# Splitting keys and weights on other engines in an attention, experts and FFN kernel

## The chip, the cores and the metric

The kernel runs on one core of one Trainium2 chip. The metric is device time in microseconds of one execution, and the median of three runs of the kernel before is 1194.65 us (1193.66 to 1194.86). The engines are TensorE (PE in the profile), VectorE (DVE), ScalarE (ACT), GpSimd (POOL) and SyncE (SP, which here only issues transfers).

## The reference

Three stages follow one another on 2304 tokens of 512 features:

```python
scores = q @ k.T / 8                      # 4 batches x 8 heads, 576 x 576, head size 64
mask = scores >= kth_largest(scores, 32)  # 32 best of each row
x = softmax(where(mask, scores, -1e9)) @ v
logits = x @ w_gate + modality_bias[modality_id]
e = argmax(logits)                        # one of 8 experts for each token
x = softmax(logits)[e] * (relu(x @ w1[e]) @ w2[e])    # 512 -> 1024 -> 512
h = x @ w_in                              # 512 -> 2048
out = where(h >= 1, h, where(h <= -1, 0, (h + 1)**2 / 4)) @ w_out
```

Everything is in 32-bit floats.

## The kernel before, in words

**Low and high parts.** TensorE multiplies a reduced form of the 32-bit floats. Where more precision is wanted, an operand is split into a high part (a copy into that form, such as `kh`, `qh`, `w1h`) and a low part (the operand less its high part: `kl`, `ql`, `w1l`), and three products stand for one.

**Attention.** The 32 heads are worked in 16 pairs, `j` = 0 to 15. Each pair has 9 units of 128 query rows by 576 keys; two units make a group, and the loop over `g` (line 504) runs through 72 groups. In a group the order of work on every engine is the order in which the Python code issues it: `topk(g)` (line 237) on VectorE and GpSimd; `masks` and `out` for the groups before; the scores of the group four later, which ScalarE evacuates from PSUM as `s`; the transposes `pt` on TensorE of the group before and their evacuations `a` on ScalarE; then what the dictionary `later` holds for this group, the first two entries of it ahead of the exponentials `e` and the others behind them.

`topk` finds the 32nd largest of each row by repeated maxima (MAX8) and replacements on VectorE. To shorten the rows it first folds them (line 207): `big`, the larger of a row's two halves, then `c` and `lit2`, the larger and smaller of the halves of `big`. One fold serves two groups and is issued in every odd group, behind that group's first maxima (lines 252, 254, 256). The third piece, `lit`, is made by GpSimd with two integer operations (`less`, line 224, its operations at 228 and 234), one group ahead; in odd groups it waits for the fold by a written-out dependency. GpSimd also makes `nm` (line 257), on which ScalarE's `e` waits, and two small copies for each group (line 241).

**Preparing a pair.** `prep(j, g)` (line 373) puts the steps of pair `j` into `later`. `turn` (line 162) transposes k or q with five TensorE transposes into a PSUM tile of the pool `sp`, of which there are two, shared with the scores; ScalarE evacuates them as `kT` or `qT`, and q a second time as `qh`. `kparts` (line 174) makes `kh` on VectorE by a cast of `kT`; `krest` and `qrest` (lines 178, 182) make `kl` and `ql` on GpSimd (for pair 0 on VectorE). Both turns come in the even group `g - 2`, `kparts` in `g - 1`, `krest` and `qrest` in the even group `g`; the loads of pair `j + 1` are issued on SP in `g - 2`.

**End of a pair.** `xout` (line 340) scales a finished pair: two small operations on VectorE (lines 345, 346), which stand behind that group's maxima, then on GpSimd `x` (line 349) and twice `xtail` (line 354). It is put into the odd group after the pair's last output.

**Routing and experts.** The tokens of the first three batches are ranked by expert inside the loop (`rank1`, `rank1_rest`), the others behind it (`rank2`, line 813); their rows are scattered to DRAM by indirect transfers that GpSimd issues. Then the experts' steps run: `up` products with w1, `down` products with w2, in an order written out in `Experts.ops`. `go(n)` issues n of them, and ahead of each one `prepare` (line 1453) issues loads on SP and the split of a weight tile two uses ahead. `split1` (line 1375) makes `w1h` on ScalarE and `w1l` on GpSimd, or on VectorE for the small steps; `split2` makes `w2h` on ScalarE and `w2l` on VectorE. The activations' parts `hh` (ScalarE) and `hl` (VectorE) follow each `up`, and the next `up` needs the one PSUM bank `h` that they read.

While the first two steps run, `route_steps` (line 850) works out on VectorE which tiles of 256 rows each later step takes. It is a generator, and between its portions one product step is issued:

```python
            for _ in self.route_steps():
                M.go(1)
```

It consists of some 60 operations on tiles of 8 to 152 columns. Behind it stands a branch on `redo` (line 605), taken when a row's 32 largest were not all found; each engine reads the flag itself. Then follow the wide steps, and the FFN, whose weights are unpacked beside them.

Of the kernel before, what the change touches and what calls it, by code (L numbers as in the profile page):

```python
# [65 lines left out]
class Kernel:  # L66
# [32 lines left out]
    def attention(self, moe):  # L99
        nc, tc = self.nc, self.tc  # L100
        with ExitStack() as ctx:
# [12 lines left out]
            def nb(n):  # L114
                return n if P.deep else 1
# [57 lines left out]

            def kparts(j):
                hi = kq["kh", j] = P.kq.tile([128, S], F32R, name="kh", bufs=nb(2))
                nc.vector.tensor_copy(hi, kq["k", j])
# [196 lines left out]
            def prep(j, g, *eng):  # L373

                at(g - 2, turn, j, "k")
                at(g - 2, turn, j, "q")
                at(g - 1, kparts, j)
                at(g, krest, j, *eng)
                at(g, qrest, j, *eng)
# [13 lines left out]
            for j in range(1, len(pairs)):  # L393
                g = odd(9 * j // 2 - AHEAD) - 1
                prep(j, g)
                if j + 1 < len(pairs):
                    at(g - 2, load, j + 1)
# [75 lines left out]
            def after(g, d):  # L473
                for j, u in units[2 * d:2 * d + 2]:
# [5 lines left out]
                    elif u == 8:  # L480
# [4 lines left out]
                        if late:  # L485
                            first.setdefault(g + 1, []).append((xout, (j,)))
                        else:
                            at(odd(g + 2), xout, j)
# [87 lines left out]
            M.copy = None  # L576
# [9 lines left out]
            M.flush()  # L586


            def again(j):
                load(j)  # L590
                load_v(j, vtile(j))
                for nm in "kq":
                    turn(j, nm)
                kparts(j)
                krest(j)
                qrest(j)
                for u in range(9):
# [84 lines left out]
    def route_consts2(self):  # L682
# [7 lines left out]
        def iota(name, shape, pattern):  # L690
            t = rp.tile(shape, F32, name=name)
            nc.gpsimd.iota(t, pattern=pattern, base=0, channel_multiplier=0,
                           allow_small_or_imprecise_dtypes=True)
            return t
# [9 lines left out]
        self.early = rp.tile([128, E], F32, name="early")  # L704
# [99 lines left out]
    def rank1_rest(self):  # L804
# [6 lines left out]
        nc.vector.tensor_scalar(j, j, self.end1[:, E - 1:E], -float(CAP), op0=ALU.subtract, op1=ALU.mult)  # L811

    def rank2(self, oh):
# [21 lines left out]
        nc.vector.tensor_copy(self.n2, cnt)  # L835
# [14 lines left out]
    def route_steps(self):  # L850
# [9 lines left out]

        k1, k2 = self.k1, self.k2
        end = row("end")
        tt(end, self.pref, k2, op=ALU.add)
        tt(end, end, self.end1, op=ALU.subtract)
        ts(end, end, self.end1[:, E - 1:E], None, op0=ALU.add)

        small = row("small")
        stt(small, k2, -float(CAP), self.n1, op0=ALU.mult, op1=ALU.add)
        yield
        tt(small, small, self.n2, op=ALU.add)  # L870
# [8 lines left out]
        def halve():  # L879

            stt(two, self.jcap, -2.0 / CAP, left[:, :, None].to_broadcast(n), op0=ALU.mult, op1=ALU.add)
            ts(two, two, 2.0, None, op0=ALU.is_ge)
# [4 lines left out]
        tt(left, left, small, op=ALU.subtract)  # L887
        halve()
        yield
        stt(odd, pairs, -2.0, left, op0=ALU.mult, op1=ALU.add)  # L890
# [4 lines left out]
        own, mate = on[:, SMALL0], on[:, SMALL0 + 1]  # L895
        tt(own, one, small, op=ALU.mult)
        tt(small, small, own, op=ALU.subtract)
        yield
        self.prefix(nth, small, "3")
# [3 lines left out]
        tt(left, last, self.early, op=ALU.subtract)  # L903
        halve()
# [8 lines left out]
        stt(rest, cover, -2.0, rest, op0=ALU.mult, op1=ALU.add)  # L913
        self.prefix(nrest, rest, "6")
        yield
# [4 lines left out]
        twice = row("twice")  # L920
        ts(twice, pairs, 2.0, None, op0=ALU.mult)
        tt(on[:, a], kk[:, a], each(twice, 2 * PAIRS), op=ALU.is_lt)
        yield
        tt(on[:, d], kk[:, d], each(rest, DYN), op=ALU.is_lt)
        stt(on[:, both], kk[:, both], 0.0, on[:, both], op0=ALU.is_ge, op1=ALU.mult)
        tt(kk[:, a], kk[:, a], each(self.early, 2 * PAIRS), op=ALU.add)
        stt(cover, cover, 2.0, self.early, op0=ALU.mult, op1=ALU.add)
        yield
        tt(kk[:, d], kk[:, d], each(cover, DYN), op=ALU.add)
        ts(kk[:, ONE0], last, -1.0, None, op0=ALU.add)  # L930
        ts(kk[:, SMALL0:], each(k2, SMALL), -1.0, None, op0=ALU.add)

        far, jump = row("far", NTAB), row("jump")
        tt(jump, end, k2, op=ALU.subtract)
        tt(jump, jump, self.base1, op=ALU.subtract)
        yield
        tt(far, kk, each(k1, NTAB), op=ALU.is_ge)
        tt(far, far, each(jump, NTAB), op=ALU.mult)
        tt(kk, kk, far, op=ALU.add)
        yield  # L940
        tt(kk, kk, each(self.base1, NTAB), op=ALU.add)
        stt(kk, kk, -float(NOCHUNK), on, op0=ALU.add, op1=ALU.mult)
        ids = fin.tile([128, 2, NTAB], F32, name="ids")
        nc.vector.tensor_reduce(ids[:, 0], kk, axis=AX.X, op=ALU.add)
        yield
# [4 lines left out]
        yield  # L950
# [336 lines left out]
class Experts:  # L1287


    def __init__(self, kn, wk, pss, steps):  # L1290
        self.kn, self.nc, self.wk, self.pss = kn, kn.nc, wk, pss
        self.steps = steps
        self.copy, self.busy, self.wide = None, False, None
# [81 lines left out]
    def split1(self, k, copy=None):  # L1375
        if k < len(self.use1):
            h, l = self.spl1[k] = [self.wk.tile([128, KC, 128], F32R, name="w1" + x, bufs=3) for x in "hl"]
            st, f = self.use1[k]
            eng = self.nc.vector if self.use1[k][0].small else self.nc.gpsimd
# [352 lines left out]
```

## Time and profile before

| | |
|---|---|
| median of 3 runs | 1194.65 us |
| profiled execution: its time / span in the profile | 1193.16 us / 1191.3 us |
| busy in the span | PE 94%, DVE 70%, ACT 59%, POOL 49% |
| mean granted TensorE clock | 0.968 of full speed |
| attention loop / routing / experts / FFN | to about 500 us / 500 to 551 / 551 to 840 / from 840 |

Times in the profile count from the first instruction of the span. A busy TensorE is not one at its peak, since ends of matmuls are modelled. In a timeline the columns are start, duration, engine, line, operation, output<-inputs with shapes; in square brackets stands the idle time of the engine ahead of the instruction, and what released it. A duration reaches a little into the next instruction, so what an instruction costs its engine is read from start to start.

### The profile page before, as it was taken

How to read it: one execution, taken by the hardware profiler on the slowest of the kernel's cores; microseconds unless marked ns; L12 is line 12 of the kernel's file. 1: busy time of each engine (PE TensorE's matmuls, PEld its weight loads, DVE VectorE, ACT ScalarE, POOL GpSimd, SP SyncE). 2: the span in 40 equal slices, each digit the busy share in tenths (PEclk: the TensorE clock that was granted, in tenths of full speed). 3: DMA queues.
4: the chain of work that ended last, by engine and by line, in shares of the span. 5: the costliest groups of instructions: out<-in, count | busy, mean ns of one | idle time of the engine just before them, and what ended most of it. 6: DMA issues, size and time to landing. Idle time of an engine off the chain costs nothing. (4 is left out here: it accounts for less than half of the span.)

```text
span 1191.3 us, 24612 instructions
## 1 busy us (share of the span) xinstructions
PE 1120.5 (94%) x8900; PEld 953.4 (80%) x8901; DVE 836.1 (70%) x2539; ACT 703.5 (59%) x1246; POOL 581.6 (49%) x668
## 2 busy tenths in 40 slices
PE   8989989999999898778999999889999999999998
PEld 5877778777887787666888777778899999999897
DVE  6999999999999999786758988488322232323222
ACT  5888989989898897633665545345433333333322
POOL 2777777777777777642324546032322323232222
PEclk7899999989999998998999999999999999999999
DMA  4036554201121003365766565242100101010000
GB/s 90 14 116 214 177 183 143 51 13 31 40 49 24 15 17 125 99 185 166 261 211 219 172 222 195 74 133 72 53 1 27 28 1 53 1 54 1 27 1 27
DMA packets 120843, 106.67 MB, mean 90 GB/s; under 512 B 64384, under 2 KB 88960, under 8 KB 120704
## 3 DMA queue, kind: packets, MB, share of 16 engines
q1 hardware_dynamic: 116320, 94.67, 25.7%
q0 software_dynamic: 2880, 9.44, 2.3%
q8 instruction: 73, 1.20, 0.4%
q10 hardware_dynamic: 1504, 0.82, 0.2%
q14 instruction: 66, 0.54, 0.2%
HBM read 70.30 MB, written 34.60 MB: 88 GB/s over the span
## 5 line engine op out<-in xcount | busy, mean ns | idle before, releaser
L1214 POOL TENSOR_TENSOR gl<-g,gh 128x384 fp32r<-128x384 f32 x96 | 97.2, 1012 | 315.9 <-ACT gh L1213 296.1
L307 PE MATMUL tp<-nhuge,w 128*128 128x128 bf16 x720 | 139.7, 229 | 18.1 <-ACT w L296 18.1
L1208 ACT ACTIVATE c<-c,half 128x384 f32<-128x384 f32 x96 | 59.2, 617 | 162.2 <-DVE c L1207 162.2
L305 PE MATMUL tp<-ident,e 128*128 128x128 f32 x720 | 152.3, 301 | 2.1 <-ACT e L291 2.0
L1207 DVE TENSOR_SCALAR c<-h 128x384 f32<-128x384 f32 x95 | 52.8, 555 | 143.1 <-PE h L1065 143.1
L1062 PE MATMUL h<-xh,wih 128*128 128x384 f32 x380 | 129.9, 342 | 5.5 <-DVEq L1118 3.2
L305 PEld LDWEIGHTS tp<-ident,e 128*128 128x128 f32 x720 | 107.6, 149 | 30.9 <-issue 9.4
L1063 PE MATMUL h<-xh,wil 128*128 128x384 f32 x380 | 129.1, 340 | 0.0
L1373 POOL TENSOR_TENSOR w1l<-w1r,w1h 128x512 fp32r<-128x512 f32 x48 | 67.9, 1417 | 121.2 <-ACT w1h L1372 88.6
L271 DVE MAX8 m<-z 128x8 f32<-128x160 f32 x432 | 117.1, 312 | 0.0
L312 ACT ACTIVATE a<-tp 128x640 f32<-128x640 f32 x144 | 102.0, 709 | 24.3 <-PE tp L307 22.9
L1073 PE MATMUL y<-woh,gl 128*128 128x512 f32 x288 | 114.7, 398 | 0.8 <-POOL gl L1214 0.8
L1071 PE MATMUL y<-woh,gh 128*128 128x512 f32 x288 | 112.7, 391 | 2.6 <-ACT gh L1213 2.3
L1211 DVE TENSOR_TENSOR g<-c,h 128x384 f32<-128x384 f32 x95 | 52.6, 553 | 88.1 <-ACT c L1208 88.1
L1072 PE MATMUL y<-wol,gh 128*128 128x512 f32 x288 | 114.2, 396 | 0.0
L291 ACT ACTIVATE e<-s,nm 128x576 f32<-128x576 f32 x144 | 103.4, 769 | 10.8 <-POOL nm L257 10.8
L296 ACT ACTIVATE w<-s,m 128x576 bf16<-128x576 f32 x144 | 103.6, 773 | 10.1 <-DVE m L271 10.1
L228 POOL TENSOR_TENSOR lit<-s 128x576 int32<-128x576 int32 x66 | 93.4, 1415 | 30.7 <-DVE lit L215 21.4
L205 ACT ACTIVATE s<-sp 128x576 f32<-128x576 f32 x144 | 93.1, 647 | 18.6 <-PE sp L197 16.3
L324 PE MATMUL tp<-v,a 128*64 128x65 f32 x2880 | 103.3, 228 | 0.1
L324 PEld LDWEIGHTS tp<-v,a 128*64 128x64 f32 x2880 | 93.0, 141 | 12.9 <-ACT a L312 5.2
L307 PEld LDWEIGHTS <-w 128*128 128x128 bf16 x720 | 81.0, 113 | 22.7 <-ACT w L296 22.6
(318 smaller groups left out, 2982.9 us busy)
## 6 DMA issues: line engine op xcount, KB each, us to landing
w1r<-in_moe_w_dram SPq DMA_DIRECT2D x56, 256.0 KB, 4.2
w2r<-in_moe_w_dram SPq DMA_DIRECT2D x56, 256.0 KB, 3.3
xs_dr<-zero SPq DMA_DIRECT2D x19, 512.0 KB, 5.3
ys_dr<-zero SPq DMA_DIRECT2D x19, 512.0 KB, 5.7
cr<-in_moe_w_in_dram SPq DMA_DIRECT2D x16, 512.0 KB, 4.8
cr<-in_moe_w_out_dram SPq DMA_DIRECT2D x16, 512.0 KB, 3.2
rows<-xs_dr SPq DMA_DIRECT2D x20, 256.0 KB, 2.8
ys_dr<-rows SPq DMA_DIRECT2D x17, 256.0 KB, 2.1
```

What stands on the lines that cost most here:

```text
L271: nc.vector.max(m8[:, i, r + 1], z[:, i])
L291: nc.scalar.activation(e, s, AF.Exp, bias=nm, scale=0.125)
L296: nc.scalar.activation(w, s, AF.Relu, bias=t, scale=-1.0)
L305: nc.tensor.matmul(o, e[:, k0:k0 + 128], self.ident, is_transpose=True, start=True, stop=False)
L307: nc.tensor.matmul(o, w[:, k0:k0 + 128], self.nhuge, start=False, stop=True)
L312: nc.scalar.activation(a, p[:, 0:640], AF.Relu)
L324: nc.tensor.matmul(o[HS[i]], a[:, k0:k0 + 64], v_[:, u % 2 if u < 8 else i, kc, :], start=kc == 0, stop=kc == 4)
L1062: nc.tensor.matmul(p, wh[c], xh[:, c, :], start=c == 0, stop=False)
L1063: nc.tensor.matmul(p, wl[c], xh[:, c, :], start=False, stop=False)
L1071: nc.tensor.matmul(y[t], hh[:, o], wh, start=first, stop=False)
L1072: nc.tensor.matmul(y[t], hh[:, o], wl, start=False, stop=False)
L1073: nc.tensor.matmul(y[t], hl[:, o], wh, start=False, stop=last)
```

## The change

The high part of the keys, `kh`, is made by ScalarE, as a second evacuation of the transposed k, and no longer by VectorE. The k turn and `krest` of a pair are issued in the odd group `g - 2`, the q turn in `g - 1`, `qrest` in the odd group `g`, where `g` is now `odd((9 * j + 1) // 2 - AHEAD - 2)`. `xout` is put ahead of what `later` already holds for its group, except for the last pairs. From `rank2` to the end of `route_steps` a flag `apart` lets VectorE make `w1l` in place of GpSimd. The step table has fewer operations, since two tiles are worked out in the first ranking and one more constant is made, and its twelve portions are cut at other places; the comparison of the halving takes one operation in place of two. In the diff two stretches of the step table, where only portions move, are left out at the line of "...".

```diff
--- before.py
+++ after.py
@@ -170,10 +170,9 @@
                 nc.scalar.activation(t, p[:, :S], AF.Copy)
                 if nm == "q":
                     nc.scalar.activation(P.Q[j % len(P.Q)][0], p[:, :512], AF.Copy)
-
-            def kparts(j):
-                hi = kq["kh", j] = P.kq.tile([128, S], F32R, name="kh", bufs=nb(2))
-                nc.vector.tensor_copy(hi, kq["k", j])
+                else:
+                    hi = kq["kh", j] = P.kq.tile([128, S], F32R, name="kh", bufs=nb(2))
+                    nc.scalar.activation(hi, p[:, :S], AF.Copy)
 
             def krest(j, eng=nc.gpsimd):
                 lo = kq["kl", j] = P.kq.tile([128, S], F32R, name="kl", bufs=nb(2))
@@ -373,9 +372,8 @@
             def prep(j, g, *eng):
 
                 at(g - 2, turn, j, "k")
-                at(g - 2, turn, j, "q")
-                at(g - 1, kparts, j)
-                at(g, krest, j, *eng)
+                at(g - 2, krest, j, *eng)
+                at(g - 1, turn, j, "q")
                 at(g, qrest, j, *eng)
 
             load(0, nc.scalar)
@@ -391,7 +389,7 @@
             at(1, self.route_consts)
             at(5, self.route_consts2)
             for j in range(1, len(pairs)):
-                g = odd(9 * j // 2 - AHEAD) - 1
+                g = odd((9 * j + 1) // 2 - AHEAD - 2)
                 prep(j, g)
                 if j + 1 < len(pairs):
                     at(g - 2, load, j + 1)
@@ -485,7 +483,8 @@
                         if late:
                             first.setdefault(g + 1, []).append((xout, (j,)))
                         else:
-                            at(odd(g + 2), xout, j)
+
+                            later.setdefault(odd(g + 2), []).insert(0, (xout, (j,)))
                         at(g + 2 - (j == final - 1) if late else g + 3, self.gate_turn, b, p)
                         if j == final - 2:
                             at(g + 3, early_logits, 0, 2)
@@ -573,7 +572,8 @@
             nc.vector.tensor_copy(lg2, acc["o"][:, 0:n2 * E].rearrange("p (t e) -> p t e", e=E))
             oh = self.one_hot(NT1, NT)
             M.go(2)
-            M.copy = None
+
+            M.copy, M.apart = None, True
             self.rank2(oh)
             loop.close()
             for t in range(NT1, NT):
@@ -584,6 +584,7 @@
                 M.go(1)
             M.go(max(2 * NFE + 3 - M.at, 0))
             M.flush()
+            M.apart = False
 
 
             def again(j):
@@ -591,7 +592,6 @@
                 load_v(j, vtile(j))
                 for nm in "kq":
                     turn(j, nm)
-                kparts(j)
                 krest(j)
                 qrest(j)
                 for u in range(9):
@@ -687,9 +687,9 @@
         nc.vector.tensor_copy(b1, bias[:, 1:2, :].to_broadcast([128, NT, E]))
         nc.vector.copy_predicated(self.btok, mi, b1)
 
-        def iota(name, shape, pattern):
+        def iota(name, shape, pattern, base=0):
             t = rp.tile(shape, F32, name=name)
-            nc.gpsimd.iota(t, pattern=pattern, base=0, channel_multiplier=0,
+            nc.gpsimd.iota(t, pattern=pattern, base=base, channel_multiplier=0,
                            allow_small_or_imprecise_dtypes=True)
             return t
 
@@ -701,7 +701,8 @@
         self.ipair = iota("ipair", [128, 2 * PAIRS, E], [[1, 2 * PAIRS], [0, E]])
         self.idyn = iota("idyn", [128, DYN, E], [[1, DYN], [0, E]])
         self.itab = iota("itab", [128, NTAB, E], [[0, NTAB], [1, E]])
-        self.early = rp.tile([128, E], F32, name="early")
+        self.early, self.from1, self.after1 = (rp.tile([128, E], F32, name=n) for n in ("early", "from1", "after1"))
+        self.jtwo = iota("jtwo", [128, E, PEREXP], [[0, E], [2, PEREXP]], 2)
         self.oh = rp.tile([128, NT + 2, E], BF16, name="oh")
         nc.vector.memset(self.oh, 0.0)
         self.mx = cst.tile([128, NT], F32, name="mx")
@@ -809,6 +810,8 @@
         j = self.jump
         nc.vector.tensor_add(j, self.end1, self.base1)
         nc.vector.tensor_scalar(j, j, self.end1[:, E - 1:E], -float(CAP), op0=ALU.subtract, op1=ALU.mult)
+        nc.vector.tensor_add(self.from1, self.base1, self.early)
+        nc.vector.tensor_scalar(self.after1, j, 1.0 / CAP, None, op0=ALU.mult)
 
     def rank2(self, oh):
         nc = self.nc
@@ -832,7 +835,7 @@
         sf = self.P.fin.tile([128, n], F32, name="sf2", bufs=1)
         nc.vector.tensor_reduce(sf, sl, axis=AX.X, op=ALU.add)
         nc.vector.tensor_copy(self.slot[:, NT1:NT], sf)
-        nc.vector.tensor_copy(self.n2, cnt)
+        nc.vector.tensor_tensor(self.n2, cnt, self.n1, op=ALU.add)
 
     def scatter(self, t):
         nc = self.nc
@@ -857,17 +860,10 @@
         def each(t, n):
             return t[:, None, :].to_broadcast([128, n, E])
 
-
-        k1, k2 = self.k1, self.k2
-        end = row("end")
-        tt(end, self.pref, k2, op=ALU.add)
-        tt(end, end, self.end1, op=ALU.subtract)
-        ts(end, end, self.end1[:, E - 1:E], None, op0=ALU.add)
+        k2 = self.k2
 
         small = row("small")
-        stt(small, k2, -float(CAP), self.n1, op0=ALU.mult, op1=ALU.add)
-        yield
-        tt(small, small, self.n2, op=ALU.add)
+        stt(small, k2, -float(CAP), self.n2, op0=ALU.mult, op1=ALU.add)
         ts(small, small, float(HALF - CAP), None, op0=ALU.is_le)
         nth = row("nth")
         on, kk = row("on", NTAB), row("kk", NTAB)
@@ -878,29 +874,31 @@
 
         def halve():
 
-            stt(two, self.jcap, -2.0 / CAP, left[:, :, None].to_broadcast(n), op0=ALU.mult, op1=ALU.add)
-            ts(two, two, 2.0, None, op0=ALU.is_ge)
+            tt(two, left[:, :, None].to_broadcast(n), self.jtwo, op=ALU.is_ge)
             nc.vector.tensor_reduce(pairs, two, axis=AX.X, op=ALU.add)
 
...
-        tt(kk[:, a], kk[:, a], each(self.early, 2 * PAIRS), op=ALU.add)
-        stt(cover, cover, 2.0, self.early, op0=ALU.mult, op1=ALU.add)
+
+        tt(kk[:, a], kk[:, a], each(self.from1, 2 * PAIRS), op=ALU.add)
         yield
+        stt(cover, cover, 2.0, self.from1, op0=ALU.mult, op1=ALU.add)
         tt(kk[:, d], kk[:, d], each(cover, DYN), op=ALU.add)
-        ts(kk[:, ONE0], last, -1.0, None, op0=ALU.add)
-        ts(kk[:, SMALL0:], each(k2, SMALL), -1.0, None, op0=ALU.add)
-
+        stt(kk[:, ONE0], last, -1.0, self.base1, op0=ALU.add, op1=ALU.add)
+        stt(kk[:, SMALL0:], each(k2, SMALL), -1.0, each(self.base1, SMALL), op0=ALU.add, op1=ALU.add)
         far, jump = row("far", NTAB), row("jump")
-        tt(jump, end, k2, op=ALU.subtract)
-        tt(jump, jump, self.base1, op=ALU.subtract)
+        tt(jump, self.pref, self.after1, op=ALU.add)
         yield
-        tt(far, kk, each(k1, NTAB), op=ALU.is_ge)
+        tt(far, kk, each(self.end1, NTAB), op=ALU.is_ge)
         tt(far, far, each(jump, NTAB), op=ALU.mult)
         tt(kk, kk, far, op=ALU.add)
-        yield
-        tt(kk, kk, each(self.base1, NTAB), op=ALU.add)
         stt(kk, kk, -float(NOCHUNK), on, op0=ALU.add, op1=ALU.mult)
         ids = fin.tile([128, 2, NTAB], F32, name="ids")
+        yield
         nc.vector.tensor_reduce(ids[:, 0], kk, axis=AX.X, op=ALU.add)
-        yield
         tt(on, on, self.itab, op=ALU.mult)
         nc.vector.tensor_reduce(ids[:, 1], on, axis=AX.X, op=ALU.add)
         ts(self.tab[:, :, 1], ids[:, 0], float(NOCHUNK), float(CAP), op0=ALU.add, op1=ALU.mult)
         nc.vector.tensor_copy(self.tab[:, :, 0], ids[:, 1])
-        yield
         ns = fin.tile([128, 1], F32, name="ns")
         nc.vector.tensor_reduce(ns, rest, axis=AX.X, op=ALU.add)
         nc.vector.tensor_copy(self.nsi[:, 0:1], ns)
@@ -1290,7 +1282,7 @@
     def __init__(self, kn, wk, pss, steps):
         self.kn, self.nc, self.wk, self.pss = kn, kn.nc, wk, pss
         self.steps = steps
-        self.copy, self.busy, self.wide = None, False, None
+        self.copy, self.busy, self.wide, self.apart = None, False, None, False
         self.count, self.late, self.jobs, self.ticks, self.xs = {}, [], [], [], {}
         ops, rest = [], []
         for n, st in enumerate(self.steps):
@@ -1376,7 +1368,7 @@
         if k < len(self.use1):
             h, l = self.spl1[k] = [self.wk.tile([128, KC, 128], F32R, name="w1" + x, bufs=3) for x in "hl"]
             st, f = self.use1[k]
-            eng = self.nc.vector if self.use1[k][0].small else self.nc.gpsimd
+            eng = self.nc.vector if st.small or self.apart else self.nc.gpsimd
             self.parts(self.raw1.pop(k), h, l, copy or self.copy, eng.tensor_tensor)
 
     def split2(self, k, copy=None, sub=None):
```

## Rows read from the trace of the kernel before

**Rows 1.** Windows by stage: length, busy us of each engine (instructions), PEclk, DMA, GB/s
```profile
26.70:431.30 404.60, 379.44 (x4722) 314.44 (x4723) 400.50 (x1628) 357.69 (x630) 306.58 (x380) 0.96 0.27 80
...
514.90:551.30 36.40, 23.90 (x136) 20.04 (x137) 28.72 (x91) 13.15 (x26) 16.16 (x18) 0.91 0.54 163
```

**Rows 2.** Waits of VectorE, 26 to 431 us: total us, times, longest
```profile
DVE c L254 <- POOL lit L234: 2.3, 11, 0.3
```

**Rows 3.** The folds by line, 26.7 to 431.3: busy us, mean ns
```profile
L213 DVE TENSOR_TENSOR big<-s 128x1152 f32<-128x1152 f32 x31 | 45.9, 1480 | 0.0
...
L214 DVE TENSOR_TENSOR c<-big 128x576 f32<-128x576 f32 x31 | 32.1, 1035 | 1.1
```

**Rows 4.** The same by source, 20 to 500 us: minimum/median/maximum ns
```profile
L213 DVE TENSOR_TENSOR big<-s x36: 753/1340/2394, 20.7 to 478.6; 128x1152 f32<-128x1152 f32 x35, 128x576 f32<-128x576 f32 x1
...
L214 DVE TENSOR_TENSOR c<-big x36: 757/758/1722, 21.5 to 480.0; 128x576 f32<-128x576 f32 x35, 128x288 f32<-128x288 f32 x1
```

**Rows 5.** Timeline of VectorE around one xout group
```profile
299.58 0.50 DVE L252 MAX8 c<-lit 128x8 f32<-128x144 f32 x2
...
307.02 0.44 DVE L176 CAST kh<-kT 128x576 fp32r<-128x576 f32 x1
307.38 0.16 DVE L345 TENSOR_SCALAR r<-xr 128x9 f32<-128x9 f32 x1
...
315.65 1.72 DVE L214 TENSOR_TENSOR c<-big 128x576 f32<-128x576 f32 x1
```

**Rows 6.** Timeline of GpSimd, same stretch
```profile
307.94 1.05 POOL L349 TENSOR_TENSOR x<-xr,r 128x512 f32<-128x512 f32 x1 [0.91 <-DVE r L346]
...
314.34 2.42 POOL L184 TENSOR_TENSOR ql<-qT,qh 128x512 fp32r<-128x512 f32 x1
```

**Rows 7.** Line 184 by source: minimum/median/maximum ns
```profile
L184 POOL TENSOR_TENSOR ql<-qT,qh x15: 1265/2384/2417, 22.7 to 431.4; 128x512 fp32r<-128x512 f32 x15
```

**Rows 8.** Timeline of ScalarE, same stretch
```profile
300.76 0.65 ACT L170 ACTIVATE qT<-sp 128x576 f32<-128x576 f32 x1
...
307.26 0.70 ACT L312 ACTIVATE a<-tp 128x640 f32<-128x640 f32 x1 [0.15 <-PE tp L307]
```

**Rows 9.** Timeline of VectorE at the start
```profile
20.36 0.46 DVE L176 CAST kh<-kT 128x576 fp32r<-128x576 f32 x1 [1.74 <-ACT kT L170]
...
21.52 1.54 DVE L214 TENSOR_TENSOR c<-big 128x288 f32<-128x288 f32 x1
```

**Rows 10.** VectorE by line, 518.95-547.24: busy us, mean ns, idle before
```profile
L1373 DVE TENSOR_TENSOR w2l<-w2r,w2h 128x512 fp32r<-128x512 f32 x6 | 4.1, 683 | 0.0
L890 DVE SCALAR_TENSOR_TENSOR odd<-pairs,left 128x8 f32<-128x8 f32 x1 | 3.5, 3550 | 0.0
L1474 DVE SCALAR_TENSOR_TENSOR hl<-h,hh 128x256 fp32r<-128x256 f32 x7 | 2.9, 420 | 1.9 <-ACT hh L1473 1.9
L925 DVE SCALAR_TENSOR_TENSOR on<-kk,on 128x128 f32<-128x128 f32 x1 | 1.4, 1400 | 0.0
...
L897 DVE TENSOR_TENSOR small<-small,on 128x8 f32<-128x8 f32 x1 | 1.1, 1146 | 0.0
L937 DVE TENSOR_TENSOR far<-kk,k 128x152 f32<-128x152 f32 x1 | 1.1, 1114 | 0.0
L946 DVE TENSOR_TENSOR on<-on,itab 128x152 f32<-128x152 f32 x1 | 1.0, 1045 | 0.0
...
L882 DVE TENSOR_SCALAR two<-two 128x72 f32<-128x72 f32 x2 | 0.4, 198 | 0.1
```

**Rows 11.** Timeline of TensorE while routing
```profile
534.40 0.58 PE L1062 MATMUL h<-xh,w1h 128*128 128x256 f32 x1 [4.57 <-DVE hl L1474]
...
551.31 0.55 PE L1063 MATMUL h<-xh,w1l 128*128 128x256 f32 x1 [2.29 <-DVEq L605]
```

**Rows 12.** GpSimd by line, 518.9 to 547.3
```profile
L1373 POOL TENSOR_TENSOR w1l<-w1r,w1h 128x512 fp32r<-128x512 f32 x7 | 8.9, 1292 | 12.2 <-ACT w1h L1372 12.2
```

**Rows 13.** Timeline of VectorE, end of the step table
```profile
547.09 0.15 DVE L953 CAST nsi<-ns 128x1 int32<-128x1 f32 x1
```

More of the change, by code (lines that the diff above doesn't have):

```diff
@@ L887, in route_steps @@
         tt(left, left, small, op=ALU.subtract)
+        yield
         halve()
+        stt(odd, pairs, -2.0, left, op0=ALU.mult, op1=ALU.add)
         yield
-        stt(odd, pairs, -2.0, left, op0=ALU.mult, op1=ALU.add)
         odds, one = row("odds"), on[:, ONE0]
@@ L895, in route_steps @@
         own, mate = on[:, SMALL0], on[:, SMALL0 + 1]
+        yield
         tt(own, one, small, op=ALU.mult)
         tt(small, small, own, op=ALU.subtract)
+        self.prefix(nth, small, "3")
         yield
-        self.prefix(nth, small, "3")
         stt(mate, nth, 0.0, small, op0=ALU.is_equal, op1=ALU.mult)
@@ L903, in route_steps @@
         tt(left, last, self.early, op=ALU.subtract)
+        yield
         halve()
@@ L913, in route_steps @@
         stt(rest, cover, -2.0, rest, op0=ALU.mult, op1=ALU.add)
+        yield
         self.prefix(nrest, rest, "6")
-        yield
         a, d = slice(PAIR0, PAIR0 + 2 * PAIRS), slice(DYN0, DYN0 + DYN)
@@ L919, in route_steps @@
         tt(kk[:, d], self.idyn, each(nrest, DYN), op=ALU.subtract)
-        twice = row("twice")
-        ts(twice, pairs, 2.0, None, op0=ALU.mult)
-        tt(on[:, a], kk[:, a], each(twice, 2 * PAIRS), op=ALU.is_lt)
         yield
+        stt(on[:, a], kk[:, a], 0.5, each(pairs, 2 * PAIRS), op0=ALU.mult, op1=ALU.is_lt)
         tt(on[:, d], kk[:, d], each(rest, DYN), op=ALU.is_lt)
         stt(on[:, both], kk[:, both], 0.0, on[:, both], op0=ALU.is_ge, op1=ALU.mult)
-        tt(kk[:, a], kk[:, a], each(self.early, 2 * PAIRS), op=ALU.add)
-        stt(cover, cover, 2.0, self.early, op0=ALU.mult, op1=ALU.add)
+        tt(kk[:, a], kk[:, a], each(self.from1, 2 * PAIRS), op=ALU.add)
         yield
+        stt(cover, cover, 2.0, self.from1, op0=ALU.mult, op1=ALU.add)
         tt(kk[:, d], kk[:, d], each(cover, DYN), op=ALU.add)
-        ts(kk[:, ONE0], last, -1.0, None, op0=ALU.add)
-        ts(kk[:, SMALL0:], each(k2, SMALL), -1.0, None, op0=ALU.add)
+        stt(kk[:, ONE0], last, -1.0, self.base1, op0=ALU.add, op1=ALU.add)
+        stt(kk[:, SMALL0:], each(k2, SMALL), -1.0, each(self.base1, SMALL), op0=ALU.add, op1=ALU.add)
         far, jump = row("far", NTAB), row("jump")
-        tt(jump, end, k2, op=ALU.subtract)
-        tt(jump, jump, self.base1, op=ALU.subtract)
+        tt(jump, self.pref, self.after1, op=ALU.add)
         yield
-        tt(far, kk, each(k1, NTAB), op=ALU.is_ge)
+        tt(far, kk, each(self.end1, NTAB), op=ALU.is_ge)
         tt(far, far, each(jump, NTAB), op=ALU.mult)
         tt(kk, kk, far, op=ALU.add)
-        yield
-        tt(kk, kk, each(self.base1, NTAB), op=ALU.add)
         stt(kk, kk, -float(NOCHUNK), on, op0=ALU.add, op1=ALU.mult)
         ids = fin.tile([128, 2, NTAB], F32, name="ids")
+        yield
         nc.vector.tensor_reduce(ids[:, 0], kk, axis=AX.X, op=ALU.add)
-        yield
         tt(on, on, self.itab, op=ALU.mult)
@@ L949, in route_steps @@
         nc.vector.tensor_copy(self.tab[:, :, 0], ids[:, 1])
-        yield
         ns = fin.tile([128, 1], F32, name="ns")
```

## The prediction

> **What bounds the kernel now.** I read the windows by stage first, then the waits of each engine, then the groups by line, then the timelines around the edited lines. The windows show two different limits [rows 1]. In the attention loop (26.7 to 431.3 us) VectorE is busy 400.5 of 404.6 us, ScalarE 357.7, GpSimd 306.6: VectorE is the bound, and in the waits it waits for one thing only, GpSimd's `lit`, 2.3 us in 11 times [rows 2]. While routing (514.9 to 551.3) no engine is full: TensorE works 23.9 of 36.4 us. After it TensorE runs nearly without a gap, and nothing there is edited, so what is won or lost before comes through to the end.
>
> Not all of VectorE's busy time is work. The `c` of a fold takes 0.76 us by its median; the mean of the 31 in the loop is 1.035, and `big` has 1.480 where its median is 1.34 [rows 3, 4]. That is 31 x 0.277 + 31 x 0.14 = 12.9 us of blocked time, about 1.0 us in each of 13 folds. The timeline of one shows why [rows 5, 6]: in an even group GpSimd runs `lit`, `kl`, `ql` back to back, `ql` is still there when the next odd group's fold begins, it stretches to 2.42 us beside `big`, and `c` takes 1.72 us. A two-input operation of VectorE and one of GpSimd exclude each other.
>
> **The change, part by part.** The sum is against the profiled execution: 1193.16 us, span 1191.3, 1.5 below the median of 1194.65; I subtract the same amount from the median.
>
> *The cast of `kh`.* Sixteen casts leave VectorE. The next operation starts 0.36 us after one (307.02 to 307.38), so 0.36 each. ScalarE takes a copy from PSUM instead; the nearest row is `qT`, the same shape and source, 0.65 us [rows 8]. At most 14 x 0.65 = 9.1 us in the loop go onto an engine with 404.6 - 357.7 = 46.9 us free: nothing, while it has that cover. Where it gives out, folds wait for evacuated scores (the start, below).
>
> *`kl` and `ql` in odd groups.* A pair's step moves as a whole: five transposes and two ScalarE copies for k (odd group), the same for q (the next even group), `kl`, `ql`, and the next pair's 8 loads on SP, which go one to two groups earlier with no wait ahead of them; TensorE gets `ql` two groups ahead of need. On GpSimd `kl` and `ql` no longer run ahead of a fold, so the 1.0 us collision goes. But writing out the group numbers of the diff, for 13 pairs (3 to 15) `ql` falls into the group of `xout`, behind `x` and `xtail` and ahead of the next `lit`. That chain has no room now: from VectorE's last operation of such a group (`x` at 307.94) GpSimd goes through to `lit`, and it is for this one that VectorE already waits, 2.3 us / 11 = 0.2 each [rows 2, 6]. An undisturbed `ql` takes 1.27 us, the shortest, where the median is 2.38 [rows 7]; a few hundredths of it lie under the next one's start, so 1.24. The wait grows from about 0.2 to about 1.45. Bounds for this new wait: 0, if GpSimd finds slack that I don't see, and 2.4, the stretched `ql`; I take 1.24, since only maxima and replacements run on VectorE then. Behind that wait stand the two `L254` maxima, the next fold and GpSimd's following `nm`; ScalarE's `e` gets its `nm` 1.24 later too, which its backlog covers. Per pair: minus 0.36, minus 1.0, plus 1.24, that is -0.12; 13 pairs: -1.5 us. Nearly the whole gain is given back.
>
> *The start.* For pair 1 VectorE idles 1.74 us until ScalarE has `kT`, then casts, and then the fold's `c` takes 1.54 us, though it is half as wide as the later ones with their 0.76, and the `lit` behind it fares alike [rows 4, 9]. The idling, 1.74, and the cast, 0.38, go, and of the blocking some 1.5; but `kl` and `ql` of pair 1 then meet the next fold (+1.0), and the first `qh` comes 0.3 later: -2.3. Pair 2 loses cast and collision without an `xout`: -1.4. Against it, ScalarE there is behind, has three copies more (2.0), and the route constants (one iota more) stand ahead of `kl` of pair 3: I keep -1.5 of the -3.7, with 0 and -3.7 as ends. Two small operations more in the first ranking cost 0.35. Attention: -1.5 - 1.5 + 0.35 = -2.6 us.
>
> *Routing.* TensorE stands still 4.57 us for `hl`, which sits on VectorE behind two portions of the step table [rows 11]. In the view by line the table's small operations take 3.55, 1.40, 1.15, 1.11 and 1.05 us where their like take 0.2, or 0.3 at the widest [rows 10]: each ran beside a `w1l` of GpSimd, seven of these in the stretch [rows 12]. With `w1l` on VectorE that blocking goes: 8.26 less 1.3 of plain work = 7.0 us. It pays seven `w1l` there, as `w2l` of the same shape 0.68 each, of which 0.08 lies under the next one's start [rows 10]: 7 x 0.60 = +4.2. The table loses nine small operations at 0.2: -1.8. That is -4.6 us of VectorE's 28. Even portions then keep VectorE within one matmul step of TensorE, so its waits for `hh` (1.9 us) [rows 10] shrink to about 0.9: -1.0. Everything ends together: VectorE's last table operation (547.09) precedes the branch on `redo`, and TensorE goes on 4.2 us after it (551.31) [rows 11, 13]; so VectorE's end counts, not TensorE's stall, and nothing else arrives later there. SP's `w1r` loads, which queue behind `w1l`, come earlier. Routing: -5.6, ends -1.8 (only the shorter table counts) and -7.8 (the portions bring one us more, the first `w1l` another).
>
> One rule speaks against this edit: the Trainium skill, page Perfetto Trace Analysis, section Optimizing Scalar/DVE Operations, warns that because VectorE and GpSimd share a read port, moving operations between the two might not help. By it the `w1l` move would be worth 0 and routing -1.8; the trace speaks against it for this stretch, since 7.0 us of blocking is exchanged for 4.2 of work.
>
> Sum: -2.6 - 5.6 = -8.2: 1185.0 for an execution like the profiled one, 1186.4 as a median.
>
> **Rivals.**
> (a) *Slower: `kl` blocks GpSimd behind a late ScalarE.* `kl` now sits on GpSimd right behind the k turn, whose copies ScalarE makes after its second `a`. In the group shown `a` ends at 307.96, 8.4 us after the group's first maximum at 299.58, while GpSimd has been free since 307.0 (`x` at 307.94, behind 0.91 idle) [rows 5, 6, 8]; adding `kT` and `kh` (1.3), `kl` would begin at 309.3, over 2 us late, and `nm` and the next `lit` stand behind it. There are 13 such groups. Nine of them come right after an `xout` group, whose wait of some 1.45 us gives the chain that much room, and ScalarE has 47 us free in the loop to catch up, so I expect little. It decides once `a` ends more than about 9 us after its group's start; with 1.2 us lost in each, 13 x 1.2 = 16: 1194.65 - 8.2 + 16 = 1202.
> (b) *GpSimd's chain has room after all.* The new wait is 0: 13 x 1.24 = 16 us more: 1170. For it: GpSimd is 76% busy (306.6 of 404.6). Against: VectorE waits there already [rows 2].
> (c) *Routing gives only the shorter table.* VectorE with `w1l` becomes as late as before, or the branch waits for another engine: 1194.65 - 2.6 - 1.8 = 1190.2. For it: VectorE is busy 28.7 of the stretch's 36.4 us already. This is also where the rule above would end up.
>
> **How the numbers follow.** Forecast 0.58, (a) 0.12, (b) 0.13, (c) 0.17. A measurement of this kernel can tell about 0.2% (2.4 us) from no change. The forecast's own range is 1182 to 1191 (routing -1.8 to -7.8, start 0 to -3.7, some of the wait). To hold 8 in 10 it reaches to (c) and part of the way to (b) and (a): 1176 to 1193. Faster: 0.58 + 0.13, and of (c) 0.10, less 0.02 of the forecast's upper end: 0.79. Same: of (c) 0.07, that 0.02 and 0.03 of (a): 0.12. Slower: the rest of (a), 0.09.
>
> **What would show it.** `c` in all folds at 0.76; VectorE's wait for `lit` near 1.4 us in 13 groups, some 19 us in all, where 2.3 stood; no `kh` on VectorE; in routing no small operation over 0.4 us after the ranking, no wait of TensorE for `hl` over 1 us, the stretch from 514.9 to the first matmul behind the branch about 30.8 us instead of 36.4. I am wrong if that wait is under 0.5 us each (b), if `kl` waits for `kh` (a), or if VectorE's last table operation comes less than 4 us earlier against the ranking (c).

## The result, and the profile after

The changed kernel took 1184.38 us, the median of 4 runs (1180.52 to 1185.88), beside 1194.76 for the kernel before on the same chip: a ratio of 0.9912, 95% interval 0.9893 to 0.9931. It is faster by 10.4 us where 8.2 were forecast (1186.4). A second set, of five executions, gave 1184.34 and 0.9918 (0.9901 to 0.9935). The profiled execution of after took 1180.52 us, the fastest of its set, and is the one read below.

The page's head and first part, and two windows (columns as in [rows 1]): attention from the first fold of group 1 to that of group 63, the stretch of [rows 1], and routing from the second ranking's first operation to the first matmul behind the branch.

```profile
span 1178.9 us, 24601 instructions
PE 1109.3 (94%) x8900; PEld 944.4 (80%) x8901; DVE 810.2 (69%) x2523; ACT 709.8 (60%) x1262; POOL 556.2 (47%) x662
```

```profile
24.74:426.05 401.31, 377.18 (x4788) 313.56 (x4789) 381.55 (x1615) 368.07 (x652) 294.26 (x384) 0.96 0.27 80
...
508.34:539.97 31.63, 22.33 (x136) 18.46 (x136) 23.83 (x89) 12.91 (x25) 6.88 (x11) 0.96 0.60 187
```

VectorE, 400.5 us busy in the loop's 404.6 before [rows 1], now has 20 us in 401 in which it does nothing. The view of its waits and that of the folds by source, 22 to 426 us, say why.

```profile
DVE c L253 <- POOL lit L233: 18.1, 13, 1.5
```

```profile
L213 DVE TENSOR_TENSOR c<-big x31: 757/758/761, 26.2 to 413.5; 128x576 f32<-128x576 f32 x31
```

```profile
L212 DVE TENSOR_TENSOR big<-s x31: 1332/1341/1348, 24.7 to 412.1; 128x1152 f32<-128x1152 f32 x31
```

The 2.3 us of [rows 2] have become 18.1 in 13 groups, 1.4 each. No `c` and no `big` of the loop is blocked any more (maximum 0.761 against the 1.72 of [rows 4]). The timelines of GpSimd and VectorE around one `xout` show the exchange.

```profile
302.06 1.04 POOL L348 TENSOR_TENSOR x<-xr,r 128x512 f32<-128x512 f32 x1 [0.53 <-DVE r L345]
303.06 0.65 POOL L353 TENSOR_TENSOR xtail<-xr,r 64x64 f32<-64x64 f32 x2
303.79 1.28 POOL L183 TENSOR_TENSOR ql<-qT,qh 128x512 fp32r<-128x512 f32 x1
...
305.47 1.41 POOL L227 TENSOR_TENSOR lit<-s 128x576 int32<-128x576 int32 x1
306.96 1.42 POOL L233 TENSOR_TENSOR lit<-lit,big 128x576 int32<-128x576 int32 x1
```

```profile
308.41 0.82 DVE L253 MAX8 c<-lit 128x8 f32<-128x288 f32 x2 [1.34 <-POOL lit L233]
```

`x`, `xtail`, `ql`, `lit` follow one another without a gap, and VectorE stands for 1.34 us, about the 1.28 of `ql`.

Routing: VectorE by line over the step table (columns as in [rows 10]), the table's last operation and the one behind the branch, and TensorE there.

```profile
L1365 DVE TENSOR_TENSOR w1l<-w1r,w1h 128x512 fp32r<-128x512 f32 x7 | 4.8, 687 | 0.0
L1365 DVE TENSOR_TENSOR w2l<-w2r,w2h 128x512 fp32r<-128x512 f32 x6 | 4.1, 684 | 0.0
L1466 DVE SCALAR_TENSOR_TENSOR hl<-h,hh 128x256 fp32r<-128x256 f32 x6 | 2.5, 420 | 2.8 <-ACT hh L1465 2.8
...
L935 DVE SCALAR_TENSOR_TENSOR kk<-kk,on 128x152 f32<-128x152 f32 x1 | 0.3, 318 | 0.0
```

```profile
535.99 0.15 DVE L945 CAST nsi<-ns 128x1 int32<-128x1 f32 x1
540.19 0.31 DVE L950 TENSOR_TENSOR lg<-lg,mx 128x144 f32<-128x144 f32 x1 [4.05 <-DVEq L605]
```

```profile
537.10 0.39 PE L1054 MATMUL h<-xh,w1h 128*128 128x256 f32 x1 [3.87 <-ACTq L605]
539.97 0.58 PE L1055 MATMUL h<-xh,w1l 128*128 128x256 f32 x1 [2.49 <-DVEq L605]
```

Where [rows 10] had small operations of 3.55, 1.40 and 1.15 us, the longest is now 0.32. The table's last operation starts 27.65 us after the ranking's first (32.18 before), the first matmul of [rows 11]'s kind 31.6 (36.4). TensorE's longest wait for `hl` in this stretch is 1.1 us, where it was 4.57 [rows 11].

The spans differ by 12.4 us. By the starts of the same operations in both, these are: up to group 1, 2.0; group 1 to 7, 2.3; group 7 to 62, 2.2; from there to the ranking, 0.1; ranking to the table's last operation, 4.5; the branch, 0.2; behind it, 1.1. The last is not the change's: a second trace of the changed kernel (e9 below) has 640.6 us behind the branch, the one read here 638.7, and the one before 639.8.

### The profile page after: what moved, and what is told of

Its sections match the earlier page's. It is cut to its first block, busy times and chain, and to the rows that moved or that the text cites. A ratio compares the mean times of both kernels' runs of the same rounds, so it can differ in the third digit from the quotient of the medians.

```text
span 1178.9 us, 24601 instructions
## 1 busy us (share of the span) xinstructions
PE 1109.3 (94%) x8900; PEld 944.4 (80%) x8901; DVE 810.2 (69%) x2523; ACT 709.8 (60%) x1262; POOL 556.2 (47%) x662
## 5 line engine op out<-in xcount | busy, mean ns | idle before, releaser
L306 PE MATMUL tp<-nhuge,w 128*128 128x128 bf16 x720 | 137.1, 227 | 20.8 <-ACT w L295 20.5
L1365 POOL TENSOR_TENSOR w1l<-w1r,w1h 128x512 fp32r<-128x512 f32 x41 | 57.7, 1408 | 124.7 <-ACT w1h L1364 98.4
L204 ACT ACTIVATE s<-sp 128x576 f32<-128x576 f32 x144 | 92.8, 648 | 10.7 <-PE sp L196 9.1
```

The costliest lines, as they stand in the source:

```text
L306: nc.tensor.matmul(o, w[:, k0:k0 + 128], self.nhuge, start=False, stop=True)
```

## The experiments

All kernels ran beside the kernel before; each time is a median, with its ratio to the kernel before and the 95% interval of that ratio. This table is worked out from the traces, of one execution each: start of group 1 and of group 7 (first maximum of `lit2`), from group 7 to 62, VectorE's waits for `lit` in that stretch, and the ranking's first operation to the table's last.

| kernel | group 1 | group 7 | 7 to 62 | waits | table |
|---|---|---|---|---|---|
| before | 25.11 | 65.2 | 359.5 | 2.0 | 32.2 |
| e7, w1l only | 23.61 | 63.8 | 359.7 | 2.2 | 28.8 |
| e8, table only | 23.27 | 62.5 | 360.2 | 2.7 | 29.9 |
| e2, routing part | 23.60 | 62.8 | 360.2 | 2.7 | 27.6 |
| e1, attention part | 23.12 | 62.8 | 357.4 | 16.9 | 32.9 |
| e12, e1 and an iota | 23.51 | 61.3 | 357.4 | 16.8 | 32.5 |
| after; again | 23.14; 23.14 | 61.0; 61.0 | 357.3; 357.2 | 16.7; 16.7 | 27.7; 27.7 |
| e4, cast only | 23.58 | 63.3 | 354.7 | 2.0 | 32.3 |
| e11, cast and routing | 23.84 | 63.9 | 355.0 | 2.0 | 27.6 |
| e3, ql even | 23.21 | 61.0 | 354.2 | 12.0 | 27.3 |
| e5, kl and ql even | 23.30 | 61.1 | 348.6 | 1.2 | 27.4 |
| e6, k early; again (e10) | 23.33; 23.13 | 61.2; 61.0 | 344.3; 345.8 | 2.0; 2.1 | 27.3; 27.7 |

### The two parts apart

e1 is the changed kernel without its routing part, e2 without its attention part. A cut of each, against the changed kernel:

```diff
-            M.copy, M.apart = None, True
+            M.copy = None
...
```

```diff
+            def kparts(j):
+                hi = kq["kh", j] = P.kq.tile([128, S], F32R, name="kh", bufs=nb(2))
+                nc.vector.tensor_copy(hi, kq["k", j])
...
```

> The kernel before with the attention part of the change alone (kh by ScalarE, krest in the odd group, qrest two groups behind it, xout first in its group); ranking, step table and w1l stay as before. If the two parts of the change add up, as I think, this gives back what the trace of after shows up to the last attention groups, 5.8 to 6.6 us: 1188 to 1189 against a kernel before of 1194.7. The rival, that the start's gain is swallowed by the slower middle before routing begins (TensorE or the scatters late there), gives under 3 us: over 1191.5. In the trace VectorE should wait for lit 18 us in 13 groups of the loop.

Measured: 1187.75 against 1193.8, ratio 0.9962 (0.9946 to 0.9978); waits as expected.

> The kernel before with the routing part alone (w1l on VectorE while routing, the shorter step table, the two tiles worked out earlier); attention as before. The traces show 36.4 us from the second ranking's first operation to the first matmul behind the branch before, and 31.6 after: if that is all, 1189.9 (4.8 less). If something behind the branch gains too, as the difference of the profiled executions (12.6, of which 11.3 stand at that matmul) may suggest, 1188 to 1189. If routing's gain needs the attention part, over 1192.

Measured: 1189.35, 0.9964 (0.9947 to 0.9981). The parts add up: 0.9962 x 0.9964 = 0.9926, within the interval of after. Each is worth about half.

### The attention part: cast or order?

e4 takes the cast off VectorE and leaves the order of `kl`, `ql` and `xout`:

```diff
+                else:
+                    hi = kq["kh", j] = P.kq.tile([128, S], F32R, name="kh", bufs=nb(2))
+                    nc.scalar.activation(hi, p[:, :S], AF.Copy)
...
-                at(g - 1, kparts, j)
```

> The kernel before with kh made by ScalarE as a second evacuation of the k transpose and nothing else: kl and ql still stand together in the even group. If the cast is worth its 0.36 us on VectorE in 14 pairs of the loop plus the 2.1 us at the start (1.74 idle, 0.38 cast), 1187.6. The collision of ql with the fold stays, so c should keep its mean of about 1.03. If GpSimd's chain takes the 0.36 back in each pair (VectorE waits that much longer for lit, since GpSimd comes no earlier), only the start is left: about 1192.5. If ScalarE's 9 us more show in the loop, 1194 or more.

Measured: 1186.9, 0.9939 (0.992 to 0.9959): by the times the cast alone gives no less than the whole attention part. Its fold, 60 to 420 us, is blocked as before:

```profile
L213 DVE TENSOR_TENSOR c<-big x28: 757/759/1728, 66.3 to 413.3; 128x576 f32<-128x576 f32 x28
```

and yet its loop is 2.7 us shorter than e1's. Its trace is of the slowest of its nine executions (1191.03): the loop's gain of 4.7 us is lost again between group 62 and the ranking, which took 94.7 us where the kernel before took 90.2. That stretch takes 89.3 to 94.7 us in the 14 traces, and 93.3 in e2 and 89.9 in e8, whose code is the same up to there; what sets it was not found. e11 is the changed kernel with this order (its edit: e4's on top of e2):

> The changed kernel without its new order of kl, ql and xout: kh by ScalarE and the whole routing part, with both turns and both low parts in the even groups of before. The loop of the kernel with the cast alone took 354.7 us, that of the changed kernel 357.3. If the new order costs what that says, 2 to 3 us less than the changed kernel: 1181.5 to 1182.5. If the order pays elsewhere (pair 2 at the start, a less late ScalarE at the loop's end), the two are equal or this one is slower: 1184 to 1187.

Measured: 1183.37, 0.9907 (0.989 to 0.9924), beside 1184.34 for the changed kernel: not to be told apart. In the table the new order loses 2.3 us in the loop (355.0 to 357.2) and wins 2.9 ahead of group 7, 2.2 of them in group 5 alone (11.0 to 8.8 us, read below). So the edit that moved most of the code, `kl` and `ql` in odd groups, brings nothing to the end that these times show.

### Is the new wait ql's?

```diff
-                at(g, qrest, j, *eng)
+                at(g + 1, qrest, j, *eng)
```

> The changed kernel with qrest one group later, in the even group behind xout's instead of in xout's group. My theory is that the 1.4 us wait of VectorE for lit in 13 groups is ql standing ahead of lit on GpSimd, and that a ql alone fits in the even group between lit and the next fold (before, kl and ql stood there together, which reached into the fold). Then the waits of VectorE for lit in the loop fall from 18.1 us to under 3, c stays at 0.76, and the time falls by 14 to 18 us from the changed kernel's 1184.4: 1166 to 1170. The rivals: the wait is not ql's but x's and xtail's, then nothing changes (1184); ql still reaches into the fold, then c and big stretch by about 1 us in 13 groups and it ends near 1182; or ScalarE, busy 368 of 402 us in the loop of the changed kernel, becomes the bound, near 1175.

Measured: 1175.88, 0.9846 (0.9814 to 0.9878), faster than the changed kernel, but 6 us short of the expectation; the waits came down to 12.0, not under 3. In the 13 groups in which the changed kernel waits 1.3 to 1.5 us, 0.3 at most are left: that wait was `ql`'s. What remains stands nearly all in seven other groups (21, 29, 35, 39, 47, 53, 57), 0.6 to 2.7 us each, and each of these follows a group in which `kl` waits for `kh`. GpSimd's timeline ahead of the first of these, and VectorE's:

```profile
146.23 1.42 POOL L179 TENSOR_TENSOR kl<-kT,kh 128x576 fp32r<-128x576 f32 x1 [3.19 <-ACT kh L175]
```

```profile
150.99 0.82 DVE L253 MAX8 c<-lit 128x8 f32<-128x288 f32 x2 [2.72 <-POOL lit L233]
```

`kl` keeps GpSimd standing for 3.19 us until ScalarE has made `kh`; in the view of its line by source that is 22.5 us in 9 times here, and 8.4 in 2 in after, both at the start. So seven times and some 14 us are new, all in the loop.

```profile
  ACT kh L175: 22.5, 9
```

```profile
  ACT kh L175: 8.4, 2
```

And ScalarE is late since TensorE is: it holds the scores back until the later `ql` is there.

```profile
137.24 0.40 PE L196 MATMUL sp<-kh,ql 64*128 64x288 f32 x1 [3.52 <-POOL ql L183]
```

```profile
138.12 0.65 ACT L204 ACTIVATE s<-sp 128x576 f32<-128x576 f32 x1 [2.80 <-PE sp L196]
...
143.46 1.56 ACT L311 ACTIVATE a<-tp 128x640 f32<-128x640 f32 x2 [0.35 <-PE tp L306]
144.96 0.65 ACT L170 ACTIVATE kT<-sp 128x576 f32<-128x576 f32 x1
145.51 0.64 ACT L175 ACTIVATE kh<-sp 128x576 fp32r<-128x576 f32 x1
```

This is rival (a) of the prediction in another kernel: `a` ends at 145.0, 9.6 us after this group's start, just beyond the 9 us named there. The time is also the one that the last rival named for a ScalarE that is full, but that is not what bounds here: ScalarE itself stands waiting for TensorE, and the next two kernels run the loop faster with the same work on ScalarE. So two ways round the late `kh` were tried: `krest` later, and the k turn earlier.

```diff
-                at(g - 2, krest, j, *eng)
+                at(g - 1, krest, j, *eng)
```

> The kernel of the experiment with qrest one group later, and krest one group later too, into the even group of the q turn, so that kh has a whole group more to arrive. There VectorE still waited 12.0 us for lit; my theory is that about 9.5 of it, in the five groups 21, 29, 35, 47 and 57, is GpSimd standing in kl for a kh that a late ScalarE had not made. Then the waits fall to about 3 us, all of them short, and the time from 1175.9 to about 1168. Rivals: kl does not end before the next fold, then c and big stretch by about 1 us in 13 groups and the time is 1177 to 1181; or TensorE and ScalarE, busy 331 and 325 of 354 us there, become the bound, then VectorE waits for s instead and it stays near 1174.

Measured: 1172.66, 0.9816 (0.9762 to 0.987), 5 us above the expectation, and by the intervals not clear of the experiment before. The waits for `lit` go (7 left, of 0.3 at most, 61 to 420 us), but the second rival has its share:

```profile
DVE big L212 <- ACT s L204: 5.3, 4, 2.1
DVE c L253 <- POOL lit L233: 1.4, 7, 0.3
```

The earlier k turn, with room for it:

```diff
-                at(g - 2, turn, j, "k")
+                at(g - 3, turn, j, "k")
...
-                    hi = kq["kh", j] = P.kq.tile([128, S], F32R, name="kh", bufs=nb(2))
+                    hi = kq["kh", j] = P.kq.tile([128, S], F32R, name="kh", bufs=3)
...
```

> The kernel with qrest one group later, and the k turn one group earlier with three buffers for kT, kh and kl; krest stays in its odd group. If the five long waits come from kl standing in front of a late kh, they go here as well, without kl near a fold: waits for lit near 3 us, 1167. If they come from ql or from xout's chain, nothing changes: 12 us of waits, 1176. If the earlier turn only makes ScalarE later for the evacuated scores, VectorE waits for s: 1174 or more.

Measured: 1171.17, 0.982 (0.9778 to 0.9861), 4 us above the expectation and no clearer of that experiment. And again, on one chip with the changed kernel:

> The changed kernel once more, beside the next two on the same chip, so that they can be compared with it: 1184.4 plus or minus 2. Its loop from group 7 to group 62 should again take 357.3 us with 18 us of waits for lit in 13 groups, and routing 27.8 us from the ranking's first operation to the table's last. What its start gains depends on TensorE's clock there: group 1 begins at 23.3 to 24 if the first 20 us run at the upper level.

> The kernel with qrest one group later and the k turn one group earlier, with three buffers, against the changed kernel on the same chip. In one look its loop took 344.3 us where the changed kernel's took 357.3. If all of that reaches the end, 1171 to 1172 against 1184.4; if late TensorE or ScalarE work at the loop's end takes part of it back, 1175 to 1178.

Measured: 1174.04 (1169.36 to 1179.03), 0.9831 (0.9807 to 0.9855), where the changed kernel had 1184.34 (1182.51 to 1185.78), 0.9918 (0.9901 to 0.9935). The intervals are apart: this version beats the kernel before by 20 us and the changed kernel by 10. Its waits from 61 to 420 us:

```profile
DVE c L253 <- POOL lit L233: 2.4, 11, 0.3
DVE big L212 <- ACT s L204: 2.3, 1, 2.3
```

Of the 12.6 us by which its group 70 starts earlier (466.98 against 479.60), 10.6 are left at the ranking: VectorE waits 4.9 us there for GpSimd's `top`, where it waited 2.5. Whether the earlier k turn does that is not shown, since e2 and e8, with one code up to there, have 4.9 and 2.5 as well. At the end of the span 8.5 are left; the 2 us behind the branch were not followed.

### Routing: w1l or the table?

e7 has the `apart` lines of the change alone, e8 the rest of its routing part:

```diff
-            M.copy = None
+            M.copy, M.apart = None, True
...
-            eng = self.nc.vector if self.use1[k][0].small else self.nc.gpsimd
+            eng = self.nc.vector if st.small or self.apart else self.nc.gpsimd
```

> The kernel before with w1l on VectorE while routing and nothing else; the step table keeps its operations and its portions. By the forecast's terms 7.0 us of blocked small operations go and 4.2 us of w1l come: VectorE's last table operation 2.8 us earlier against the ranking's first operation, 29.5 us instead of 32.3, and 1191 against 1193.8. The rival, that moving operations between the two engines gives nothing because VectorE pays in work what it paid in blocking, leaves 32.3 and 1193.8. A third, that VectorE, now with all the splits in the old uneven portions, holds TensorE up longer, gives 34 and 1195 or more.

Measured: 1189.45, 0.9979 (0.9959 to 0.9999), and 28.8 us where 29.5 were expected.

> The kernel before with the shorter step table in its new portions alone; w1l stays on GpSimd. By the forecast's terms nine operations fewer at 0.2 us: 1.8 us, 30.5 instead of 32.3 us from the ranking's first operation to the table's last, with operations of 1 us and more still there beside each w1l; 1192. If the new portions are what counts, and the blocked operations now meet w1l less often, 28 us and 1189.5, as with both edits. If what is left is blocked all the same, 32 and 1193.8.

Measured: 1191.24, 0.9984 (0.9963 to 1.0006), not to be told from no change by the times, and 29.9 where 30.5 were expected. VectorE by line in e8's routing still has the blocked operations, at other places:

```profile
L752 DVE TENSOR_TENSOR pre<-odd,lt 128x64 f32<-128x64 f32 x1 | 3.2, 3198 | 0.0
...
L933 DVE TENSOR_TENSOR far<-far,jump 128x152 f32<-128x152 f32 x1 | 1.3, 1259 | 0.0
L752 DVE TENSOR_TENSOR pre<-small,lt 128x64 f32<-128x64 f32 x1 | 1.2, 1174 | 0.0
```

In the traces e7 gains 3.4 us of 32.2, e8 2.2, both together 4.5 and not 5.6. Added up from start to start, VectorE's work shrinks as forecast: in e7 7.1 us of blocking go and 4.2 of `w1l` come, and after has 1.9 less again for nine operations fewer. Of the missing 1.1 us 0.9 are idle time of VectorE, 0.6 less in e7 and e8 together and 0.3 more in after, whose waits for `hh` are 2.8 us where they were 1.9: it now runs ahead of TensorE.

### Group 5

In the changed kernel group 5 takes 8.8 us, in e1, with the same attention, 10.6. In it VectorE makes the route constants beside GpSimd's. The one thing that the routing part adds there is an iota ahead of `kl`:

```diff
+        self.jtwo = iota("jtwo", [128, E, PEREXP], [[0, E], [2, PEREXP]])
```

> The kernel with the attention part alone and one iota more on GpSimd, a spare one, after the others of the route constants. Group 5, in which VectorE makes its own route constants, took 10.7 us before, 10.6 with the attention part alone and 8.8 in the changed kernel. My theory: the iota that the routing part adds holds kl of pair 3 off the copies of VectorE in this group, so that the 1.1 and 1.4 us operations there become 0.4 and 0.3; then this group takes 8.8 us here too. The rival, that the shorter group is one execution's luck or comes of other parts of the routing edit, leaves 10.6.

Measured, in one execution: 8.77 us. VectorE in e1 and in e12:

```profile
55.39 1.13 DVE L685 COPY b<-bias 128x144 f32<-128x144 f32 x1
56.55 1.44 DVE L686 COPY_PREDICATED btok<-mi,b 128x144 f32<-128x144 int32 x1
```

```profile
55.79 0.42 DVE L685 COPY b<-bias 128x144 f32<-128x144 f32 x1
56.24 0.32 DVE L686 COPY_PREDICATED btok<-mi,b 128x144 f32<-128x144 int32 x1
```

In e1 `kl` runs from 56.41, so that the second of these operations lies beside it; in e12 it begins at 57.03, behind them. So an instruction that does nothing useful goes with 1.8 us here, and the group takes 8.8 us in all seven traces that have it in the new order. Holding `kl` off can account for 1.1 of them, the second operation. The first one is slower in e1 as well, beside the same iotas, and that happens elsewhere: in before, e4, e7 and e11, where `kl` and `ql` are done well before, the copy `mi` ahead of these two takes 1.52 to 1.77 us while GpSimd runs nothing but iotas, and 0.40 to 0.42 in the other ten traces. In before:

```profile
58.36 1.52 DVE L685 COPY mi<-mod 128x144 int32<-128x144 int32 x1
```

e11 has the added iota too. When iotas hold up a copy and when not stays open, and with it whether the added one cured the rest of the 1.8 us or e1 was one unlucky execution.

## Why the prediction was right, and where not

**Range and likeliest case: right.** 1184.4 lies in it, 2.0 below the forecast. That the sum comes so near is luck in part: 2.6 us were forecast for attention and 5.6 for routing, and e1 and e2 gave 4.5 and 4.3. Their intervals (2.6 to 6.4 and 2.3 to 6.3 us) still reach to both forecasts, but the traces say the same: too little for the start, too much for routing.

**The 13 pairs, -1.5: right, -2.2.** Cast -0.36, collision -1.0, wait +1.24 were the three terms. e4's loop is 4.7 us shorter than before: 13 x 0.36 = 4.7. e1's is 2.7 longer than e4's, that is +0.2 a pair for wait less collision, as forecast (0.24). From group 7 to 62, which holds 12 of the 13 collisions, 11.9 us of blocking in `c` and `big` go from e4 to e1 and 14.7 of waits come: 1.0 and 1.2 a pair, the forecast's sizes. Rival (b), a GpSimd with room, is out: the wait is 1.4. Rival (a) is out for this order (in after `kl` waits for `kh` at the start only) and became real as soon as `ql` moved.

**The start, -1.5: mis-sized; measured -4.3 in the profiles, and for another reason.** The 1.74 us of idling before the cast [rows 9], counted as the change's to take away, were TensorE's clock. Windows of the first 25 us, before and e8, whose attention is the same code:

```profile
0.00:25.00 25.00, 22.39 (x100) 14.60 (x103) 14.67 (x43) 11.83 (x19) 5.34 (x15) 0.74 0.45 96
```

```profile
0.00:25.00 25.00, 19.44 (x107) 11.81 (x109) 16.40 (x50) 13.13 (x22) 5.57 (x15) 0.96 0.44 96
```

From 15 to 20 us the granted clock is 0.50 in before (the level of 1.2 GHz) and 1.00 (2.4 GHz) in all 13 other traces; until about 12 us TensorE had done about the same work at the upper level in before and e8. At a granted 0.74 group 1 starts at 25.1, at 0.96 at 23.3; in e2, e7 and e8, all with the old start, it is 23.3 to 23.6 and the idling is not there. So some 1.5 to 1.8 of the 2.0 us up to group 1 are the luck of one execution, and what is left is about the cast. The Trainium skill, page TensorE: Matmul & The Clock Gate, section Part 1: The HAM clock gate (the "warmup" mystery), says that how long the start of one and the same kernel runs at the lower clock changes from run to run; these traces agree. Nor did the `c` of pair 1 get shorter: 1.54 us in both, so the 1.5 of blocking put down there did not go. From group 1 to 7 it is 2.3 us, where the forecast had 1.4 for pair 2: about 0.4 for its cast (group 3) and 1.9 for group 5. In group 5 the collision of pair 2 went as forecast, 1.0 us, before and after:

```profile
51.45 2.37 DVE L213 TENSOR_TENSOR big<-s 128x1152 f32<-128x1152 f32 x1
```

```profile
49.13 1.34 DVE L212 TENSOR_TENSOR big<-s 128x1152 f32<-128x1152 f32 x1
```

The other 0.9 is the copies beside the iotas, for which the forecast had no term. In e1 the copies cost 0.9 more than before instead, and nearly the whole gain is taken back (10.7 to 10.6 us). ScalarE's delay, for which the term was held at -1.5, did not show.

**Routing, -5.6: right in kind, 4.8 by the matmul.** In e7 7.0 of blocking against 4.2 of `w1l` should give 2.8 and gave 3.4; in e8 nine operations should give 1.8 and gave 2.2. The step that failed is the smallest: VectorE's waits for `hh` were to shrink by 1.0 and grew by 0.9. The rule weighed there, that moving work between VectorE and GpSimd might not help (the Trainium skill, page Perfetto Trace Analysis, section Optimizing Scalar/DVE Operations), does not hold in this stretch by e7: 32.2 to 28.8 us. Rival (c) is out.

**+0.35 for the first ranking: 0.2.** The two operations stand in group 66. Groups 66 and 67 together take 14.1 us in the five traces without them and 14.3 in the nine with them.

## What to carry to other kernels

A collision between two engines that is cured by moving one operation is paid where that operation then stands: look for the slot that is free on the engine moved and on the one behind it, here the even group for `ql` alone, and an earlier source for `kl`. Split a change along its edits before believing in any of them; here the times do not tell the cast alone from the cast with the new order, which moved most of the code. An idle time at the start of one execution is no term of a sum before a second execution of the same code shows it.

## What was not expected of the hardware

Not every instruction of GpSimd blocks VectorE alike: COPY_PREDICATED took 1.44 us beside `kl` and 0.32 beside iotas. The Trainium skill, page SBUF — State Buffer, section SBUF: two separate sides, says that a VectorE operation with two inputs in SBUF excludes only an operation of GpSimd that reads SBUF; an iota reads none, and this pair of rows agrees. A plain COPY fares otherwise: `mi`, with one input, took 1.52 to 1.77 us beside iotas alone in four traces and 0.40 to 0.42 in ten. Getting past the branch that is not taken keeps VectorE standing for 3.7 to 4.4 us, in all 14 traces.
